# Weight loads of 1, 2 and 1 MB, and the sinks' rows of v from on-chip copies and late loads, in a fused window attention and gated MLP kernel

## The chip, the cores and the metric

The kernel runs on one core of a Trainium2 chip. The metric is device time in microseconds (us) of one execution; lower is better. Times are medians of several executions; the profile comes from one further execution with the hardware profiler on.

## The reference

Attention with a causal window of 128 keys plus 4 "sink" keys at the start of the sequence, over 4 batches, 8 heads, 768 positions and a head size of 64, all float32. Its output, laid out as 3072 tokens by 512, goes through an MLP with a gate.

```python
scores = scale * np.matmul(q, k.transpose(0, 1, 3, 2))
is_sink = pos[None, :] < int(n_sink)
rel = pos[:, None] - pos[None, :]
in_window = (rel >= 0) & (rel < int(window))
scores = np.where(is_sink | in_window, scores, -1000000000.0)
a = np.exp(scores - np.max(scores, axis=-1, keepdims=True))
a = a / (np.sum(a, axis=-1, keepdims=True) + 1e-09)
attn = np.matmul(a, v)
...
x = attn.transpose(0, 2, 1, 3).reshape(B * S, H * D)
h = x @ w_in                       # 3072 x 512 times 512 x 2048
g = h * (1.0 / (1.0 + np.exp(-beta * h)))
out = g @ w_out                    # 2048 x 512
```

## The kernel before, in words

**Units and tiles.** A unit n is one pair of heads over half a sequence (384 queries); there are 32. Four units make a tile of 384 tokens by 512 columns (xT), and there are 8 tiles, two to a batch. For each tile the MLP has 16 blocks of 128 hidden columns. A block is four matmuls (`hidden_matmul`, L814), a tanh on ACT (L822) and a gate on DVE (L835). `project` (L843) then multiplies each block by w_out for three groups of 128 tokens; it can run for two groups at a time.

**A unit's steps.** q and k arrive and are transposed; scores are matmuls (L700, or L727 for later units); the exponential is on ACT (L707, L735), the mask on DVE (L714, L741). In the second half of a sequence the four sink keys lie outside the window for all queries, so there is a separate score matmul against `k_sink` (L670), its exponential `E_sink`, and a matmul with `v_sink` (L759), whose rows 0 to 3 and 32 to 35 hold the first four rows of v for the two heads of the pair. `attend` also multiplies by v (L770), `normalise` makes the reciprocal `rden` (L779) and `o_norm` (L781), and `transpose_out` gives xT.

**Loads.** Each issuing engine has a queue of its own. SP issues q and k of units 0 to 11 as float32 (`load_qk`, L522). ACT issues v of batch 0, first half (L528). GpSimd (POOL) issues all loads that convert float32 to bf16 on the way: w_in in four loads of 1 MB (512 hidden columns each, source rows of 2 KB, L578), w_out in eight of 0.5 MB (L583), the sinks' rows of k (L592) and of v for all batches (two loads of 8 KB, L596), v by half batches (`load_v`, L542), and, from unit 12 on, q, k and v by pair (`land_qk` L552, `land_v` L561). POOL also casts most of the first q, k and v (L621, L532), fills `k_sink` and makes the masks.

**What waits for what around the change.** A load of w_in signals once, at its end; a block that uses any column of it waits for that. `load_qk` for units 4 to 7 waits for the second w_in load. `load_qk` for units 8 to 11 waits for w_out loads (blocks 4, 6, 8 and 10), and `load_v` for batch 1 for other w_out loads. An attention of a second half waits for `v_sink`.

**Order.** The program is written as a list of operations with their reads and writes. A planner (`Prog.order`) works out from given costs (`busy`, `lag`, for a transfer its size over a rate, a `late` offset and a weight for sharing) when each could start, and from that writes one fixed order per engine. Each engine then goes through its order and waits on semaphores; what stands behind a waiting instruction waits too. So a changed cost changes no instruction, but it can change the order. `AGENDA` says at which step (one MLP block is one step) a unit's parts are put on the list, and `products` how many project matmuls a step gets.

Of the kernel before, what the change touches and what calls it, by code (L numbers as in the profile page):

```python
# [9 lines left out]
B, H, S, D = 4, 8, 768, 64  # L10
# [45 lines left out]
AGENDA = {}  # L56
for n in range(4, 8):
    for step, at in (("in", n - 4), ("sink", 16), ("a", 16), ("b", 16), ("av", 17), ("out", 18)):
        AGENDA.setdefault(at if step == "in" else at + 1 * (n - 4), []).append((n, step))
for n in range(8, NU):  # L60
    for at, step in STEPS.items():
        AGENDA.setdefault(FIRST[n] + at, []).append((n, step))
# [294 lines left out]
def bass_streamingllm_window__then__act_swish_beta_kernel(  # L357
# [159 lines left out]
    def load_qk(n, x, after=(), queue="sp"):  # L517
        _, _, half, pb = place(n)
        name = "qk"[x]
        s = rows_of((q, k)[x], n, 1, half, 3)  # L520
        d = stage[name][pb][:, :, 3 * half:3 * half + 3, :].rearrange("p h c d -> p h (c d)")
        op(queue, lambda e: e.dma_start(d, s), w=[(name + "_stage", pb, half)], after=after,  # L522
           dma=f"{name}{pb}_{half}", seq="loads " + queue, **transfer(2 * TT * D * 4, 290 if n not in (1, 2) or x else 170, 520.0))

    def load_v32(x, c):

# [49 lines left out]
    def load_w_in(m, ms, after=()):  # L576
        here = slice(m * 128, (m + ms) * 128)
        op("gp", lambda e: e.dma_start(w_in16[:, :, here], w_in_src[:, :, here]), after=after,  # L578
           w=[("w_in", c, mm) for c in range(4) for mm in range(m, m + ms)],
           dma=f"wi{m}", late=0.0 if m else 800.0, **transfer(DM * ms * 128 * 4, 385, 740.0, 3.0))  # L580

    def load_w_out(m, ms, after=()):
        op("gp", lambda e: e.dma_start(w_out16[:, m:m + ms, :], w_out_src[:, m:m + ms, :]), after=after,  # L583
           w=[("w_out", mm) for mm in range(m, m + ms)],
           dma=f"wo{m}", **transfer(ms * 128 * NOUT * 4, 416, 740.0, 3.0))

    def load_sinks(x, after=()):
        for hh in range(2):
            rows = slice(HEAD1 * hh, HEAD1 * hh + NSINK)
            if x:  # L590
                src = k[:, :, 0:NSINK, :].rearrange("b (g h) s d -> h (b g) s d", h=2)[hh]
                op("gp", lambda e, hh=hh, src=src: e.dma_start(k_rows[:, :, hh, :], src),  # L592
                   w=[("k_rows", hh)], after=after, dma=f"sk{hh}", busy=650.0, lag=300.0, weight=0.4)
            else:
                src = v[:, :, 0:NSINK, :].rearrange("b (g h) s d -> s h (b g) d", h=2)[:, hh]
                op("gp", lambda e, rows=rows, hh=hh, src=src: e.dma_start(v_sink[rows, :, hh, 0:D], src),  # L596
                   w=[("v_sink", hh)], r=["v_sink"], after=after, dma=f"sv{hh}", busy=650.0, lag=400.0, weight=0.4)

    def sink_keys():

# [144 lines left out]
    def attend(n, av_ps=av_ps, name="av"):  # L745
# [9 lines left out]
        with P.together("pe"):  # L755
            for mm in range(3):
                m, at = 3 * half + mm, mm * 2 * D1
                if half == 1:
                    op("pe", lambda e, at=at, mm=mm: e.matmul(  # L759
                        av_ps[:, at:at + 2 * D1], E_sink[z][:, mm * 128:mm * 128 + 128],  # L760
                        v_sink[:, n // 8 * 4 + hp, :, :].rearrange("p h e -> p (h e)"),
                        start=True, stop=False, skip_group_check=True),
                       r=[("E_sink", z), "v_sink", ("v_sink", 0), ("v_sink", 1)], w=[name],
                       **pe(130))
                for hh in range(2):
                    kbs = range(m + 1) if half == 0 else (m - 1, m)
                    for x, kb in enumerate(kbs):
                        col = 128 * where[kb, m]
                        op("pe", lambda e, at=at, hh=hh, kb=kb, col=col, first=(half == 0 and x == 0),
                           last=(x == len(kbs) - 1): e.matmul(  # L770
                            av_ps[:, at + hh * D1:at + hh * D1 + D1], E[z][:, hh, col:col + 128],
                            v_aug[:, pb, hh, kb, 0:D1], start=first, stop=last, skip_group_check=True),
                           r=[("E", z, 0), ("E", z, 1), ("v", pb, kb, hh), ("v_ones", pb)],
                           w=[name], **pe(65))
# [101 lines left out]
    load_w_in(0, 4, [("v", 0, 0, 0)])  # L876
    cast_v(1)
    cast(2)
    load_sinks(1, [("v", 1, 0, 0)])

    select(ident32[:, :], ones32[:, :], [[1, 32]], ALU.is_equal, 0.0, 0, -1, ["ones32"], ["ident32"])
    transpose_first(0)
# [10 lines left out]
    transpose_first(1)  # L893
    first_scores(0)
    cast(3)
    load_w_in(4, 4, [("k16", 0)])
    cast_v(2)
    load_w_in(8, 4, [("v", 2, 0, 0)])
    cast_v(3)
    load_w_in(12, 4, [("v", 3, 0, 0)])  # L900
    for n in range(4):
# [2 lines left out]
        if n < 3:  # L904
            first_scores(n + 1)
        if n == 2:
            for y in range(4, 8):
                for x in range(2):
                    load_qk(y, x, [("w_in", 0, 4)])
            fill("gp", k_sink[:, :, :], 0.0, ["k_sink"], busy=1800.0, after=[("v", 3, 0, 0)])  # L910
            masks([("v", 3, 0, 0)])
            load_sinks(0, [("v", 3, 0, 0)])
            for c in range(3):
                load_v(1, c, [("v", 3, 0, 0)])
            load_w_out(0, 2, [("v", 3, 0, 0)])
# [2 lines left out]
        normalise(n, *bank)  # L918
    for n in range(4):
        transpose_out(n, s_ps[:, n % 2, :], f"s{n % 2}", "dve" if n in (0, 3) else "act")  # L920
    for i in range(2):
        with P.together("pe"):
            for c in range(3):
# [14 lines left out]
    for s in range(-2, S_END + NM):  # L938
# [39 lines left out]
                load_v(2, c, [("w_out", 2 * c + 6)])  # L978
        if s == 23:
            load_v(2, 2)  # L980
        if s in lands:
            for x in range(2):
                land_qk(lands[s], x, [("rden", 0)])
# [57 lines left out]
```

## Time and profile before

| what | value |
|---|---|
| three runs | 229.0 us median, 228.53 to 230.1 |
| the profiled execution's own time | 228.59 us |
| its span, first to last instruction | 226.9 us |
| granted clock of TensorE | 1.0 |
| busy: PE, DVE, ACT, POOL | 220.0, 132.6, 141.3, 125.7 us |
| POOL's waits for a reciprocal before land loads (L552) | 24.0 us, 9 times |
| time to landing, w_in loads: min, median, max | 5.5, 6.8, 9.8 us |
| time to landing, v_sink loads | 7.8 and 7.9 us |
| time to landing, w_out loads: min, median, max | 8.9, 9.6, 11.3 us |

The profile comes from one execution. PE is TensorE's matmul, PEld its weight load, DVE the vector engine, ACT the scalar engine, POOL GpSimd, SP the sync engine; a "q" behind the name means that engine's sequencer, which issues transfers. Times are us from the span's start. A row of the timeline has start, length, engine, source line, operation, tiles as out<-in, the shape and the count; in brackets stands how long the engine was idle before it and what released it. A DMA row on an engine is the issue; the time to landing is counted from that issue to the end of the transfer. A row of stages has its stretch, then busy us and instructions of each engine, the granted clock, the mean share in which the core's 16 DMA engines were busy (over 1 where packets of several queues overlap) and GB/s.

### The profile page before, as it was taken

How to read it: one execution, taken by the hardware profiler on the slowest of the kernel's cores; microseconds unless marked ns; L12 is line 12 of the kernel's file. 1: busy time of each engine (PE TensorE's matmuls, PEld its weight loads, DVE VectorE, ACT ScalarE, POOL GpSimd, SP SyncE). 2: the span in 40 equal slices, each digit the busy share in tenths (PEclk: the TensorE clock that was granted, in tenths of full speed). 3: DMA queues.
4: the chain of work that ended last, by engine and by line, in shares of the span. 5: the costliest groups of instructions: out<-in, count | busy, mean ns of one | idle time of the engine just before them, and what ended most of it. 6: DMA issues, size and time to landing. Idle time of an engine off the chain costs nothing.

```text
span 226.9 us, 4463 instructions
## 1 busy us (share of the span) xinstructions
PE 220.0 (97%) x1761; PEld 122.1 (54%) x1761; DVE 132.6 (58%) x264; ACT 141.3 (62%) x224; POOL 125.7 (55%) x191
## 2 busy tenths in 40 slices
PE   7999989999999999999999999999999999999995
PEld 4665545555555555555555555555555555555454
DVE  5466777488975776566565656555656564443200
ACT  1877796197586877566657766666656755555311
POOL 4689992899994979695939396876300000000000
PEclk9999999999999999999999999999999999999999
DMA  6999999999998999999999999998921012110122
GB/s 172 251 172 179 276 194 205 257 228 139 118 138 124 124 117 151 120 167 144 116 113 135 99 138 147 96 165 119 94 80 53 20 57 64 49 46 0 58 83 92
DMA packets 96901, 28.92 MB, mean 127 GB/s; under 512 B 83424, under 2 KB 93936, under 8 KB 96880
## 3 DMA queue, kind: packets, MB, share of 16 engines
q0 software_dynamic: 59232, 10.92, 65.7%
q1 hardware_dynamic: 34304, 16.79, 34.3%
q10 hardware_dynamic: 3344, 0.93, 1.9%
q8 instruction: 14, 0.23, 0.5%
q14 instruction: 7, 0.06, 0.1%
HBM read 27.34 MB, written 6.29 MB: 148 GB/s over the span
## 4 chain that ended last, share of the span: by engine, by line
PE 73%; DMA 15%; POOL 8%; issue 2%; SPq 1%; ACT 0%; POOLq 0%; ACTq 0%
PE acc L843 32%; PE h_ps L814 29%; DMA k_stage<-in_k_dram 8%; DMA w_out<-in_moe_w_out_dram 4%; PE s_ps L727 4%; PE s_ps L770 4%; POOL qk L621 3%; DMA w_in<-in_moe_w_in_dram 2%; POOL land L552 2%; PE h_ps L843 2%; POOL v_aug L561 1%; PE s_ps L759 1%; PE s_ps L670 1%; SPq L522 1%; POOL v_aug L532 0%
## 5 line engine op out<-in xcount | busy, mean ns | idle before, releaser
L822 ACT ACTIVATE th<-h_ps,beta_half 128x384 f32<-128x384 f32 x120 | 69.4, 581 | 59.7 <-PE h_ps L814 59.1
L843 PE MATMUL acc<-w_out,g 128*128 128x512 bf16 x368 | 99.7, 380 | 0.0
L814 PE MATMUL h_ps<-xT,w_in 128*128 128x384 bf16 x480 | 96.2, 326 | 0.0
L835 DVE SCALAR_TENSOR_TENSOR g<-th,h_ps 128x384 bf16<-128x384 f32 x120 | 65.6, 550 | 44.8 <-ACT th L822 44.0
L814 PEld LDWEIGHTS h_ps<-xT,w_in 128*128 128x128 bf16 x480 | 45.6, 98 | 39.8 <-issue 0.8
L843 PEld LDWEIGHTS acc<-w_out,g 128*128 128x128 bf16 x368 | 32.8, 98 | 28.8 <-issue 3.6
L552 POOL DMA_DIRECT2D land<-in_q_dram x40 | 30.2, 760 | 24.0 <-DVE rden L779 24.0
L552 POOL DMA_DIRECT2D land<-in_k_dram x40 | 30.3, 761 | 0.0
L561 POOL DMA_DIRECT2D v_aug<-in_v_dram x40 | 30.2, 760 | 0.0
L735 ACT ACTIVATE E<-s_ps 128x1536 bf16<-128x1536 f32 x20 | 28.8, 1442 | 0.0
L741 DVE TENSOR_TENSOR E<-E,mask 128x1536 bf16<-128x1536 bf16 x20 | 19.2, 958 | 16.4 <-ACT E L735 16.4
L851 ACT ACTIVATE out_sb<-acc 128x512 f32<-128x512 f32 x23 | 13.7, 596 | 7.6 <-PE acc L843 7.4
L770 PEld LDWEIGHTS s_ps<-v_aug,E 128*128 128x128 bf16 x336 | 15.2, 97 | 3.2 <-issue 1.2
L770 PE MATMUL s_ps<-v_aug,E 128*128 128x65 bf16 x336 | 16.8, 193 | 0.0
L707 ACT ACTIVATE E<-s_ps 128x768 bf16<-128x768 f32 x17 | 13.7, 811 | 4.3 <-PE s_ps L700 4.2
L781 DVE TENSOR_TENSOR o_norm<-s_ps,rden 128x384 bf16<-128x384 f32 x28 | 15.6, 556 | 0.8
L714 DVE TENSOR_TENSOR E<-E,mask 128x768 bf16<-128x768 bf16 x16 | 9.0, 572 | 2.0 <-ACT E L707 1.3
L727 PE MATMUL s_ps<-qkT 64*128 64x256 bf16 (+2 forms) x144 | 10.1, 254 | 0.0
L759 PE MATMUL s_ps<-v_sink,E_sink 128*128 128x130 bf16 x48 | 9.3, 219 | 0.0
L621 POOL CAST qk<-k_stage 128x384 bf16<-128x384 f32 x12 | 6.5, 544 | 4.7 <-DMA k_stage<-in_k_dram 4.4
L673 ACT ACTIVATE E_sink<-s_ps 128x384 bf16<-128x384 f32 x16 | 7.8, 490 | 1.5 <-PE s_ps L670 1.5
L727 PEld LDWEIGHTS s_ps<-qkT 64*128 64x128 bf16 x144 | 4.9, 94 | 7.1 <-issue 5.8
(75 smaller groups left out, 155.2 us busy)
## 6 DMA issues: line engine op xcount, KB each, us to landing
out_dram<-out_sb SPq DMA_DIRECT2D x23, 256.0 KB, 2.7
q_stage<-in_q_dram SPq DMA_DIRECT2D x12, 192.0 KB, 7.4
k_stage<-in_k_dram SPq DMA_DIRECT2D x12, 192.0 KB, 7.9
w_in<-in_moe_w_in_dram POOLq DMA_DIRECT2D x4, 512.0 KB, 6.8
w_out<-in_moe_w_out_dram POOLq DMA_DIRECT2D x8, 256.0 KB, 9.6
land<-in_q_dram POOLq DMA_DIRECT2D x40, 48.0 KB, 3.7
land<-in_k_dram POOLq DMA_DIRECT2D x40, 48.0 KB, 4.0
v_aug<-in_v_dram POOLq DMA_DIRECT2D x40, 48.0 KB, 3.4
```

The lines of the kernel that those rows point to most:

```text
L552: op("gp", lambda e, d=d, s=s: e.dma_start(d, s), w=[("land", pb, half, x, hh)], after=after, dma=f"l{pb}{half}{x}{hh}", **transfer(TT * D ...
L561: op("gp", lambda e, d=d, s=s: e.dma_start(d, s), w=[("v", pb, 3 * half + c, hh) for c in range(3)], after=after, dma=f"lv{pb}{half}{hh}", ...
L707: op("act", lambda e: e.activation(both, src[:, :, 0:TT], AF.Exp, bias=0.0, scale=SCALE), x=list(names), w=[("E", n % NE, c)], **act(768))
L727: op("pe", lambda e, at=at, w=w, kb=kb, qb=qb, nq=nq, hh=hh, rows=rows, bank=bank: e.matmul(s_ps[:, 2 * hh + bank, at:at + w], keys_of(pb, ...
L735: op("act", lambda e: e.activation(E[z][:, :, :], src, AF.Exp, bias=0.0, scale=SCALE), x=list(S_NAMES), w=[("E", z, 0), ("E", z, 1)], **ac ...
L741: op("dve", lambda e: e.tensor_tensor(E[z][:, :, :], E[z][:, :, :], m.unsqueeze(1).to_broadcast([128, 2, 768]), ALU.mult), r=[("E", z, 0), ...
L770: last=(x == len(kbs) - 1): e.matmul(av_ps[:, at + hh * D1:at + hh * D1 + D1], E[z][:, hh, col:col + 128], v_aug[:, pb, hh, kb, 0:D1], sta ...
L781: op("dve", lambda e: e.tensor_tensor(o_norm[o][:, :, :, :].rearrange("p m h d -> p (m h) d"), src[:, :, 0:D], rden[z][:, :].unsqueeze(2). ...
L814: op("pe", lambda e: e.matmul(bank, w_in16[:, c, m * 128:(m + 1) * 128], xT[:, c, T * TT:(T + 1) * TT], start=(c == 0), stop=(c == 3)), r= ...
L822: op("act", lambda e: e.activation(th[i % 3][:, :], bank, AF.Tanh, bias=0.0, scale=beta_half[:, m:m + 1]), x=[name], r=["beta"], w=[("th", ...
L835: op("dve", lambda e: e.scalar_tensor_tensor(g[T % 2][:, m, :], th[i % 3][:, :], 1.0, bank, ALU.add, ALU.mult), r=[("th", i % 3)], x=[name ...
L843: op("pe", lambda e: e.matmul(bank[:, 0:width], g[T % 2][:, m, t * 128:(t + 1) * 128], w_out16[:, m, cols], start=(m == 0), stop=(m == NM ...
```

## The change

The w_in loads become 1, 2 and 1 MB: blocks 0 to 3, blocks 4 to 11 in one load whose source rows are 4 KB, and blocks 12 to 15. The middle load is issued where the second one was. `load_qk` for units 4 to 7 stands later in the program, and still waits for the load that holds block 4, which is now the one of 2 MB. The two loads of the sinks' rows of v for all batches go. For batches 0 and 1, DVE copies the rows from `v_aug`, where v already lies, to `v_sink` (two copies of four partitions by 256 elements for each batch; batch 1 at step 34). For batches 2 and 3, POOL loads them at steps 48 and 80, two small loads each. The sinks' rows of k are loaded as before. Some costs that the planner is given change: the rate of two q loads, the rates of the w_in loads, and the `late` offset of the first.

```diff
--- before.py
+++ after.py
@@ -56,7 +56,7 @@
 AGENDA = {}
 for n in range(4, 8):
     for step, at in (("in", n - 4), ("sink", 16), ("a", 16), ("b", 16), ("av", 17), ("out", 18)):
-        AGENDA.setdefault(at if step == "in" else at + 1 * (n - 4), []).append((n, step))
+        AGENDA.setdefault(at if step == "in" else at + n - 4, []).append((n, step))
 for n in range(8, NU):
     for at, step in STEPS.items():
         AGENDA.setdefault(FIRST[n] + at, []).append((n, step))
@@ -520,7 +520,7 @@
         s = rows_of((q, k)[x], n, 1, half, 3)
         d = stage[name][pb][:, :, 3 * half:3 * half + 3, :].rearrange("p h c d -> p h (c d)")
         op(queue, lambda e: e.dma_start(d, s), w=[(name + "_stage", pb, half)], after=after,
-           dma=f"{name}{pb}_{half}", seq="loads " + queue, **transfer(2 * TT * D * 4, 290 if n not in (1, 2) or x else 170, 520.0))
+           dma=f"{name}{pb}_{half}", seq="loads " + queue, **transfer(2 * TT * D * 4, 290, 520.0))
 
     def load_v32(x, c):
 
@@ -577,24 +577,36 @@
         here = slice(m * 128, (m + ms) * 128)
         op("gp", lambda e: e.dma_start(w_in16[:, :, here], w_in_src[:, :, here]), after=after,
            w=[("w_in", c, mm) for c in range(4) for mm in range(m, m + ms)],
-           dma=f"wi{m}", late=0.0 if m else 800.0, **transfer(DM * ms * 128 * 4, 385, 740.0, 3.0))
+           dma=f"wi{m}", late=0.0 if m else -600.0,
+           **transfer(DM * ms * 128 * 4, 308 if m > 4 else 360, 740.0, 3.0))
 
     def load_w_out(m, ms, after=()):
         op("gp", lambda e: e.dma_start(w_out16[:, m:m + ms, :], w_out_src[:, m:m + ms, :]), after=after,
            w=[("w_out", mm) for mm in range(m, m + ms)],
            dma=f"wo{m}", **transfer(ms * 128 * NOUT * 4, 416, 740.0, 3.0))
 
-    def load_sinks(x, after=()):
+    def load_sink_keys(after=()):
+        for hh in range(2):
+            src = k[:, :, 0:NSINK, :].rearrange("b (g h) s d -> h (b g) s d", h=2)[hh]
+            op("gp", lambda e, hh=hh, src=src: e.dma_start(k_rows[:, :, hh, :], src),
+               w=[("k_rows", hh)], after=after, dma=f"sk{hh}", busy=650.0, lag=300.0, weight=0.4)
+
+    def sink_values(b, eng, after=()):
+
         for hh in range(2):
             rows = slice(HEAD1 * hh, HEAD1 * hh + NSINK)
-            if x:
-                src = k[:, :, 0:NSINK, :].rearrange("b (g h) s d -> h (b g) s d", h=2)[hh]
-                op("gp", lambda e, hh=hh, src=src: e.dma_start(k_rows[:, :, hh, :], src),
-                   w=[("k_rows", hh)], after=after, dma=f"sk{hh}", busy=650.0, lag=300.0, weight=0.4)
-            else:
-                src = v[:, :, 0:NSINK, :].rearrange("b (g h) s d -> s h (b g) d", h=2)[:, hh]
-                op("gp", lambda e, rows=rows, hh=hh, src=src: e.dma_start(v_sink[rows, :, hh, 0:D], src),
-                   w=[("v_sink", hh)], r=["v_sink"], after=after, dma=f"sv{hh}", busy=650.0, lag=400.0, weight=0.4)
+            op(eng, lambda e, rows=rows, hh=hh: e.tensor_copy(
+                v_sink[rows, 4 * b:4 * b + 4, hh, 0:D], v_aug[0:NSINK, :, hh, 0, 0:D]),
+               r=["v_sink", *(("v", z, 0, hh) for z in range(4))], w=[("v_sink", b, hh)],
+               busy=200.0, lag=140.0, after=after)
+
+    def load_sink_values(b):
+        for hh in range(2):
+            rows = slice(HEAD1 * hh, HEAD1 * hh + NSINK)
+            src = v[b, :, 0:NSINK, :].rearrange("(g h) s d -> s h g d", h=2)[:, hh]
+            op("gp", lambda e, rows=rows, hh=hh, src=src: e.dma_start(
+                v_sink[rows, 4 * b:4 * b + 4, hh, 0:D], src),
+               w=[("v_sink", b, hh)], r=["v_sink"], after=[("rden", 0)], dma=f"sv{b}{hh}", busy=650.0, lag=400.0, weight=0.4)
 
     def sink_keys():
 
@@ -760,7 +772,7 @@
                         av_ps[:, at:at + 2 * D1], E_sink[z][:, mm * 128:mm * 128 + 128],
                         v_sink[:, n // 8 * 4 + hp, :, :].rearrange("p h e -> p (h e)"),
                         start=True, stop=False, skip_group_check=True),
-                       r=[("E_sink", z), "v_sink", ("v_sink", 0), ("v_sink", 1)], w=[name],
+                       r=[("E_sink", z), "v_sink", ("v_sink", n // 8, 0), ("v_sink", n // 8, 1)], w=[name],
                        **pe(130))
                 for hh in range(2):
                     kbs = range(m + 1) if half == 0 else (m - 1, m)
@@ -876,7 +888,7 @@
     load_w_in(0, 4, [("v", 0, 0, 0)])
     cast_v(1)
     cast(2)
-    load_sinks(1, [("v", 1, 0, 0)])
+    load_sink_keys([("v", 1, 0, 0)])
 
     select(ident32[:, :], ones32[:, :], [[1, 32]], ALU.is_equal, 0.0, 0, -1, ["ones32"], ["ident32"])
     transpose_first(0)
@@ -893,9 +905,8 @@
     transpose_first(1)
     first_scores(0)
     cast(3)
-    load_w_in(4, 4, [("k16", 0)])
+    load_w_in(4, 8, [("k16", 0)])
     cast_v(2)
-    load_w_in(8, 4, [("v", 2, 0, 0)])
     cast_v(3)
     load_w_in(12, 4, [("v", 3, 0, 0)])
     for n in range(4):
@@ -904,12 +915,9 @@
         if n < 3:
             first_scores(n + 1)
         if n == 2:
-            for y in range(4, 8):
-                for x in range(2):
-                    load_qk(y, x, [("w_in", 0, 4)])
             fill("gp", k_sink[:, :, :], 0.0, ["k_sink"], busy=1800.0, after=[("v", 3, 0, 0)])
             masks([("v", 3, 0, 0)])
-            load_sinks(0, [("v", 3, 0, 0)])
+            sink_values(0, "dve")
             for c in range(3):
                 load_v(1, c, [("v", 3, 0, 0)])
             load_w_out(0, 2, [("v", 3, 0, 0)])
@@ -918,6 +926,9 @@
         normalise(n, *bank)
     for n in range(4):
         transpose_out(n, s_ps[:, n % 2, :], f"s{n % 2}", "dve" if n in (0, 3) else "act")
+    for n in range(4, 8):
+        for x in range(2):
+            load_qk(n, x, [("w_in", 0, 4)])
     for i in range(2):
         with P.together("pe"):
             for c in range(3):
@@ -978,6 +989,10 @@
                 load_v(2, c, [("w_out", 2 * c + 6)])
         if s == 23:
             load_v(2, 2)
+        if s == 34:
+            sink_values(1, "dve", [("rden", 1)])
+        if s in (48, 80):
+            load_sink_values(2 if s == 48 else 3)
         if s in lands:
             for x in range(2):
                 land_qk(lands[s], x, [("rden", 0)])
```

## The prediction

> **What bounds the kernel now.** I read the table by stages first, with its granted clock, then the chain that ended last, then TensorE's and GpSimd's order of time, and last the time to landing of single transfers (a tile's view, narrowed to one issue). Columns of the stages: busy us and instructions of PE, PEld, DVE, ACT, POOL; granted clock; DMA share and GB/s.
>
> ```profile
> 15.00:20.00 5.00, 4.99 (x64) 3.52 (x61) 2.79 (x8) 3.29 (x8) 4.70 (x12) 1.00 1.17 175
> 20.00:25.00 5.00, 5.00 (x32) 2.99 (x32) 4.35 (x9) 4.46 (x9) 5.00 (x11) 1.00 1.17 242
> 25.00:30.00 5.00, 4.59 (x36) 2.42 (x33) 4.05 (x8) 3.51 (x7) 4.88 (x9) 1.00 1.48 245
> 30.00:35.00 5.00, 3.69 (x50) 1.94 (x48) 3.89 (x8) 5.00 (x9) 4.40 (x8) 1.00 1.55 196
> 35.00:40.00 5.00, 5.00 (x62) 2.99 (x58) 3.32 (x8) 2.96 (x5) 0.89 (x1) 1.00 1.24 204
> ```
> The clock is full. TensorE is the bound nearly everywhere after 15 us; the hole that this change can reach is 25 to 35 us, and there the DMA share is 1.48 and 1.55: the DMA engines, not the issuing engines, are full.
>
> ```profile
> 12.45 5.50 DMA w_in<-in_moe_w_in_dram
> 17.96 0.37 SPq L522
> 18.37 7.79 DMA k_stage<-in_k_dram
> ...
> 27.81 9.58 DMA w_out<-in_moe_w_out_dram
> 37.41 0.37 SPq L522
> 37.82 7.45 DMA k_stage<-in_k_dram
> ```
> In the chain the reader is to see that from 12.5 to 45 us transfers alone carry the end: the second weight load lands at 17.95, releases the loads of q and k for units 4 to 7, then w_out (block 4) at 37.39 releases those for units 8 to 11. After 60 us the chain is TensorE and nothing else.
>
> ```profile
> 19.26 1.51 PE L814 MATMUL acc<-xT,w_in 128*128 128x384 bf16 x8
> ...
> 24.51 1.76 PE L814 MATMUL acc<-xT,w_in 128*128 128x384 bf16 x8
> ...
> 34.81 0.34 PE L700 MATMUL h_ps<-qkT 64*128 64x128 bf16 x4 [0.36 <-ACT E L707]
> 35.08 1.04 PE L843 MATMUL acc<-w_out,g 128*128 128x512 bf16 x4
> ```
> Matmuls of L814 start 0.163 us apart, so a block (four) is 0.65. Block 3 starts at 19.26 and block 4, the first that needs the second load, at about 19.9. The second of the two rows from 24.51 on holds block 12's wait for the fourth load (the waits of this window: 0.5 us, once). The first project matmul comes at 35.08.
>
> ```profile
> 12.45 0.76 POOL L578 DMA_DIRECT2D w_in<-in_moe_w_in_dram  x1 [0.30 <-POOL qk L621]
> 14.02 0.74 POOL L578 DMA_DIRECT2D w_in<-in_moe_w_in_dram  x1 [0.30 <-POOL v_aug L532]
> 15.57 0.74 POOL L578 DMA_DIRECT2D w_in<-in_moe_w_in_dram  x1 [0.30 <-POOL v_aug L532]
> 20.92 1.29 POOL L596 DMA_DIRECT2D v_sink<-in_v_dram  x2
> 22.20 2.68 POOL L542 DMA_DIRECT2D v_aug<-in_v_dram  x3
> 24.85 0.74 POOL L583 DMA_DIRECT2D w_out<-in_moe_w_out_dram  x1
> ```
> GpSimd's own queue. Issue plus time to landing gives, in order: w_in 14.4, 17.95, 21.9 and 25.4; v_sink 28.7 and 29.5; v_aug 32.0, 32.8 and 33.6; w_out 34.9, then 36.1 and 37.4. So one stream serves them one behind the other.
>
> **The part before 35 us that is empty.** TensorE's block 15 is through at 28.9 (28.26 plus four times 0.163). From there to 35.08 are 6.2 us, and the starts of the rows in it hold: three sets of six transposes, 0.35 each; six sets of scores, 0.27 each; two sink scores, 0.16 each; one unit's attention, 0.57. That is 3.6 us of work, so 2.6 us are empty for want of w_out, while ACT is busy for 5.00 of 5.00.
>
> **The change, part by part.**
>
> *Second w_in load of 2 MB.* One issue on POOL goes (0.74 and the 0.30 ahead of it: 1.04 us), so everything behind it on POOL moves up by that: the last w_in issue, the fill of k_sink, the masks, v_aug, w_out. None is short of its issue (each lands 8 to 10 us after it), so 0 to the end. What the larger load adds is a wait: blocks 4 to 11 now need all of it. Two loads of 1 MB took from 14.4 to 21.9 (7.5 us); w_out, same rows, lands 0.5 MB of source each 1.28 us, which is 5.1 us for 2 MB. So it lands between 19.6 and 21.9; I take 20.7, about the middle, since no q and k transfers run beside it any more. Block 4 wants it at 19.9: +0.8 us (0 to +2.0) behind which every later block queues. Block 12 loses its wait: −0.5. Block 15 ends 0.3 later, by itself inside the 2.6 empty us, if what follows is not late as well.
>
> The row length is a size for a rule. Spacings of landings are 3.5, 4.0 and 3.5 us per MB although each load takes 5.5 to 9.8 from issue; start-up costs thus lie beside the load in front. The Trainium skill, DMA: Bandwidth & Descriptors, section "Anatomy of one DMA — SWDGE (gpsimd) path", gives about 2.0 us fixed per transfer plus bytes over 436 GB/s. By that, one transfer fewer is 2 us less of stream; by the spacings it is nothing, and I go by the spacings. The result by the rule is the third rival.
>
> *Loads of q and k, units 4 to 7.* They wait for that same load, so SP issues the first at 20.7 and not at 17.96, +2.7. Nothing else waits in SP's queue then (the next is 37.4), so their place in the program is worth 0. They landed first at 25.2 and last at 31.9 (22.52 plus 9.4). The first landing was as late as the fourth w_in load's, 25.4: the engines had been giving themselves to weights. With no q and k beside it that load ends sooner, by about 1 us (four spacings of 3.5 would end at 24.9, at w_out's rate at 22.1). So I take 0 for the landings, ends −0.5 and +2.7 (each time from issue kept as it is).
>
> *v_sink off the queue.* POOL loses 2 issues, 1.29 us: 0, as above. In the stream, the two of 8 KB stand between 25.4 and 29.5, 4.06 us. If that is theirs alone, v_aug and w_out come 4.06 earlier; if the engines were at q and k meanwhile (share 1.48), nothing is won, for those bytes still have to move. Seven of the eight landings of q and k fall in 25.4 to 31.9, so the second is the nearer row: I take 1.0 of the 4.06. First w_out at 33.9, and the project matmuls after it fill what was empty: −1.0 (0 to −2.6, all that is empty). What is late next is w_out's own stream: 1.28 us for two blocks, against four project matmuls of 0.21.
>
> *Two copies of v's rows on DVE for batch 0, two for batch 1.* Nearest row: an xT copy of 384 columns takes 0.35; these have 256, from 4 partitions: 0.25 each. The first two need the last v cast (15.3 now, about 14.2 after), and DVE idles 1.16 us up to 15.24 and 0.51 before 17.52; if they slip behind that, o_norm and so the last xT move by up to 0.5. The other two fall at step 34, where DVE is busy 6.5 of 10 us but TensorE waits for its gate (0.7 us, 3 times in all). Cover gone, 0.5 each; I take +0.2 for both pairs (0 to +1.0).
>
> *Four late DMAs of v_sink rows, steps 48 and 80.* 0.65 each, 1.3 per pair, on POOL, behind a reciprocal that the land loads wait for too. POOL idles 1.3 to 3.8 us there once a unit (24.0 in all, waiting for rden), and land loads come units ahead: 0, or 1.3 late on one unit's loads if that idle is not there.
>
> *The planner's numbers* (rate 290 for q of units 1 and 2, lateness −600, rates 360 and 308) change no instruction, only the order on each engine. Not seen here; bounds ±0.5, one unit's wait like those of 0.5 above; 0 taken.
>
> **Sum.** −1.0 (w_out earlier) +0.3 (block 15 later, taken whole) +0.2 (DVE) = −0.5. The profiled execution took 228.59 (span 226.9 and 1.7 around it), 0.4 under the median 229.0 of the three and at their lower edge: 228.59 − 0.5 = 228.1.
>
> **Rivals.**
>
> *The queue time is really v_sink's.* For: 16 KB can't need 4.06 us of a stream that moves 0.5 MB in 1.28. Against: the share of 1.48. Then w_out starts at about 30.8 and three pairs of blocks, 12 matmuls of 0.21, fill the 2.6 us: 228.59 − 2.6 + 0.3 = 226.3.
>
> *Slower: q and k come late.* Issue moves 2.7 us and landings follow. ACT is full from 29.2 to 36, each unit's cast follows its k within 0.1 us, so there is no slack at the last unit. Work of units 5 to 7 that is now done before 35.08 (two sets of transposes 0.70, four of scores 1.08, a sink score 0.16) then falls behind w_out's arrival: +2.0, with the copies +0.2: 230.8. It decides once k of unit 4 lands after about 27.3 (its cast, transposes and copy take 2 us and block 15 ends at 29.2). For: 2.7 us is more than the 1.1 us that unit 4 has to spare. Against: the first landing has followed the weights, not the issue. The Trainium skill, same page, section "Queues, rings and completion order", has each engine go round its queues by packet, so v_aug, no longer held behind v_sink, would take turns with q and k from the start. By that alone the spacing of q and k landings, 0.95 us, would stretch; in the trace the last three, with v_aug landing beside them, come 0.8 to 1.0 apart, so it does not show.
>
> *Fixed costs are saved.* Stream 2 us shorter: the large load lands at 19.9, block 4 does not wait, block 12's 0.5 goes: 228.59 − 1.0 − 0.5 + 0.2 = 227.3.
>
> **How the numbers follow.** Forecast 0.45, queue time 0.18, late q and k 0.22, fixed costs 0.15. About 1% (2.3 us) is what a measurement can tell from no change. Faster by more than that: the first rival and little else, 0.20. Slower by more: the second rival lies at 1%, so half of it and a little for several ends at once, 0.13. Within: 0.67. The likeliest alone has 227.0 to 229.4; the 8 in 10, reaching to both outer rivals, is 226.0 to 230.9.
>
> **What would show it.** Second w_in landing 6 to 6.5 us after the first and a wait for it at block 4 of 0.5 to 1; no wait at block 12; k of unit 4 landing within 1 us of 26.2; first w_out at 33 to 34.5, first project matmul right behind; the stages 25 to 35 with about 1 us more busy TensorE; stages after 70 us unchanged but for a shift. Wrong if the first project matmul is not earlier, or if TensorE's order before 17 us differs by more than 0.5 us.

## The result, and the profile after

The changed kernel takes 234.26 us (median of six runs, 233.75 to 235.85) against 229.06 for the kernel before (six runs, 227.92 to 230.1): a ratio of 1.0237, with a 95% interval of 1.0205 to 1.0269. It is slower by 5.2 us, outside the range of 226.0 to 230.9. The profiled execution took 233.98 (span 232.2), so the comparison of the two traces has 5.3 us of span to explain. In the experiments below, three of the ten executions of the weights alone (its profiled one among them, 235.3 to 237.5) and one of the eight with the old rate (238.4) lie far above the others of their kernel and are left out of the ratios.

Most lines move by 12: MLP hidden L826, project L855, transposes L646, scores L712, attention L771 and L782, cast L633; the w_out load moves by 1, to L584. The stages of the kernel after, in the same columns:

```profile
15.00:20.00 5.00, 4.99 (x69) 3.31 (x70) 2.50 (x9) 3.44 (x7) 4.73 (x12) 1.00 1.04 178
20.00:25.00 5.00, 5.00 (x32) 2.91 (x31) 3.71 (x7) 4.36 (x8) 5.00 (x9) 1.00 1.28 202
25.00:30.00 5.00, 4.61 (x34) 2.70 (x31) 4.20 (x9) 3.62 (x8) 4.41 (x8) 1.00 1.59 239
30.00:35.00 5.00, 2.58 (x28) 1.39 (x26) 3.25 (x6) 4.29 (x7) 1.11 (x4) 1.00 1.22 229
35.00:40.00 5.00, 3.00 (x27) 1.99 (x29) 1.30 (x4) 2.00 (x4) 3.39 (x6) 0.53 1.24 206
```

From 30 to 40 us TensorE is busy for 5.58 of 10 us, where it was 8.69 before, and from 35 to 40 the granted clock is 0.53. From 15 to 30 us its busy time is as before. All of the loss is there when tile 1 of the MLP begins, at 51.67 and not at 44.51 (7.2 us); 1.9 us of it are made good by the last matmul (229.22 against 223.92). The chain of waits, narrowed to the first 45 us, shows what TensorE stood behind:

```profile
13.26 8.08 DMA w_in<-in_moe_w_in_dram
21.34 0.02 issue
21.35 0.37 SPq L522
...
24.99 11.65 DMA k_stage<-in_k_dram
36.64 0.05 issue
36.70 0.52 POOL qk L633
37.22 0.05 issue
37.26 0.50 PE s_ps L646 x3
...
39.83 1.06 PE acc L855 x2
```

The 2 MB load lands at 21.34, releases SP's loads of q and k, and the last of these (k of unit 7) is issued at 24.99 and lands at 36.64. Then come a cast, the transposes, the scores and the attention ahead of it in TensorE's order, and only then the first project matmul, at 39.83 and not at 35.08. TensorE's own order:

```profile
33.39 0.33 PE L712 MATMUL h_ps<-qkT 64*128 64x128 bf16 x4
35.72 0.48 PE L646 MATMUL s_ps<-ident,qk 128*128 128x128 bf16 x3 [2.01 <-POOL qk L633]
37.26 0.50 PE L646 MATMUL s_ps<-ident,qk 128*128 128x128 bf16 x3 [1.06 <-POOL qk L633]
...
39.83 1.06 PE L855 MATMUL acc<-w_out,g 128*128 128x512 bf16 x2 [0.22 <-issue]
```

The two waits are for the casts of q and k of unit 7. The project matmul has nothing to wait for any more: the first w_out load was issued at 23.27 and landed at 33.9. It stands behind unit 7, and TensorE does not go round it. GpSimd's order shows what was put ahead of the late loads:

```profile
20.64 2.66 POOL L542 DMA_DIRECT2D v_aug<-in_v_dram  x3
23.27 3.54 POOL L584 DMA_DIRECT2D w_out<-in_moe_w_out_dram  x5
26.75 0.57 POOL L633 CAST qk<-q_stage 128x384 bf16<-128x384 f32 x1
...
34.95 0.63 POOL L633 CAST qk<-q_stage 128x384 bf16<-128x384 f32 x1 [2.07 <-DMA q_stage<-in_q_dram]
35.52 0.70 POOL L584 DMA_DIRECT2D w_out<-in_moe_w_out_dram  x1
36.70 0.51 POOL L633 CAST qk<-k_stage 128x384 bf16<-128x384 f32 x1 [0.48 <-DMA k_stage<-in_k_dram]
```

Before, v_aug was issued at 22.20, four microseconds behind the first q (17.96), and w_out, but for its last three loads, one at a time between casts (24.85 to 33.8). Now v_aug goes at 20.64, ahead of the first q (21.35), and five w_out loads follow in one row.

An issue is not yet a first packet. Before, the first q was issued at 17.96 and its first packet moved at 21.60; from 18 to 21 us one queue alone shows packets, that of the weights:

```profile
q0 software_dynamic: 533, 0.53, 112.4%
```

So in packets q and k start only 1.75 us later in the kernel after (23.35 against 21.60), where the issue moved by 3.4. The larger shift is v_aug's: its first packet moves at 23.01, ahead of all of q and k; before, no packet of v_sink or v_aug moved until 25.09.

**How the queues share the DMA engines.** q and k of units 4 to 7 are 8 loads of 256 packets of 768 bytes, on the queue named hardware_dynamic; v_aug (128-byte packets) and the weights (1 KB, 2 KB in the merged load) are on software_dynamic. The transfer view gives packets, MB and share for a stretch. Before, 24 to 25 us, q and k all but alone:

```profile
q1 hardware_dynamic: 413, 0.30, 91.9%
q0 software_dynamic: 36, 0.03, 18.4%
```

After, 31 to 33 us, beside w_out:

```profile
q0 software_dynamic: 282, 0.26, 76.7%
q1 hardware_dynamic: 283, 0.21, 41.5%
```

In one of the experiments (q and k released earlier), 25 to 29 us, beside v_aug:

```profile
q1 hardware_dynamic: 1150, 0.83, 85.0%
q0 software_dynamic: 1150, 0.15, 55.3%
```

Packet for packet: 283 to 282, and 1150 to 1150. q and k move 413 packets per us nearly alone, 288 beside v_aug and 142 beside w_out, whose packets are longer. It is not one to one everywhere: from 24 to 27 us in the kernel after it is 657 of q and k to 1593 of the other queue, 219 per us, which is slower still for q and k; this was not resolved further. So it matters how many of the 2048 are through before the others join. The rule of the Trainium skill, DMA: Bandwidth & Descriptors, section "Queues, rings and completion order", is that each engine goes round its queues by packet. The prediction had set it aside; two of the three stretches beside another queue agree with it, and the third, 657 to 1593, does not.

A share over 1 is no measure of a full rate: before, 24 to 25 us moved 330 GB/s at a share of 1.10, and 28 to 32 us, mostly v_aug, 192 GB/s at 1.88. So the shares of 1.48 and 1.55 from which the prediction called the DMA engines full do not show it by themselves.

### The profile page after: what moved, and what is told of

Read it like the earlier page. It is cut to its first block, busy times and chain, and to the rows that moved or that the text cites. A ratio compares the mean times of both kernels' runs of the same rounds, so it can differ in the third digit from the quotient of the medians.

```text
span 232.2 us, 4436 instructions
## 1 busy us (share of the span) xinstructions
PE 219.8 (95%) x1730; PEld 122.4 (53%) x1757; DVE 133.3 (57%) x268; ACT 141.7 (61%) x224; POOL 127.1 (55%) x192
## 4 chain that ended last, share of the span: by engine, by line
PE 82%; DMA 11%; POOL 2%; issue 1%; SPq 1%; ACTq 1%; ACT 0%; POOLq 0%
PE acc L855 35%; PE h_ps L826 32%; DMA k_stage<-in_k_dram 5%; PE s_ps L782 5%; PE s_ps L739 4%; DMA w_in<-in_moe_w_in_dram 3%; DMA v_stage<-in_v_dram 3%; PE h_ps L855 2%; SPq L522 1%; PE s_ps L712 1%; PE s_ps L771 1%; PE s_ps L682 1%; PE s_ps L646 1%; PE s_ps L810 1%; POOL qk L633 1%
## 5 line engine op out<-in xcount | busy, mean ns | idle before, releaser
L855 PE MATMUL acc<-w_out,g 128*128 128x512 bf16 x341 | 95.4, 382 | 1.5 <-issue 0.5
L826 PE MATMUL h_ps<-xT,w_in 128*128 128x384 bf16 x480 | 96.4, 326 | 0.1
L826 PEld LDWEIGHTS h_ps<-xT,w_in 128*128 128x128 bf16 x480 | 45.5, 98 | 39.4 <-issue 1.0
L855 PEld LDWEIGHTS acc<-w_out,g 128*128 128x128 bf16 x368 | 33.1, 98 | 29.4 <-issue 4.5
L552 POOL DMA_DIRECT2D land<-in_q_dram x40 | 30.6, 767 | 21.9 <-DVE rden L791 21.9
L782 PE MATMUL s_ps<-v_aug,E 128*128 128x65 bf16 x336 | 17.2, 195 | 0.1
L782 PEld LDWEIGHTS s_ps<-v_aug,E 128*128 128x128 bf16 x336 | 15.6, 98 | 3.1 <-issue 1.3
L791 DVE RECIPROCAL rden<-s_ps 128x6 f32<-128x6 f32 x28 | 5.4, 193 | 8.6 <-PE s_ps L782 8.4
L771 PE MATMUL s_ps<-v_sink,E_sink 128*128 128x130 bf16 x48 | 9.6, 223 | 0.0
L633 POOL CAST qk<-k_stage 128x384 bf16<-128x384 f32 x12 | 6.7, 559 | 5.1 <-DMA k_stage<-in_k_dram 5.1
L646 PE MATMUL s_ps<-ident,qk 128*128 128x128 bf16 x48 | 5.0, 230 | 4.6 <-POOL qk L633 4.1
```

The costliest lines, as they stand in the source:

```text
L552: op("gp", lambda e, d=d, s=s: e.dma_start(d, s), w=[("land", pb, half, x, hh)], after=after, dma=f"l{pb}{half}{x}{hh}", **transfer(TT * D ...
L782: last=(x == len(kbs) - 1): e.matmul(av_ps[:, at + hh * D1:at + hh * D1 + D1], E[z][:, hh, col:col + 128], v_aug[:, pb, hh, kb, 0:D1], sta ...
L826: op("pe", lambda e: e.matmul(bank, w_in16[:, c, m * 128:(m + 1) * 128], xT[:, c, T * TT:(T + 1) * TT], start=(c == 0), stop=(c == 3)), r= ...
L855: op("pe", lambda e: e.matmul(bank[:, 0:width], g[T % 2][:, m, t * 128:(t + 1) * 128], w_out16[:, m, cols], start=(m == 0), stop=(m == NM ...
```

## The experiments

**Theories.** *Late q and k:* the release by a load that ends at 21 instead of 18 lets v_aug and w_out be there first; q and k then move at 142 to 288 packets per us, where they had 413, and TensorE waits in order behind unit 7. *The load itself:* one signal for 2 MB holds blocks 4 to 11, and block 15 ends later. *The clock:* the half clock from 35 us on is the loss. *The start:* the planner's new numbers put TensorE's first work in a worse order.

**The parts one by one.** Three runs of the kernel before with one part each. The rate alone:

```diff
-290 if n not in (1, 2) or x else 170, 520.0
+290, 520.0
```

> The kernel before with one planner number of the change alone: the rate of the q loads of units 1 and 2 is 290, not 170. No load and no instruction differs, only the order. Theory A (transfers: q and k of units 4 to 7 land up to 4.8 us late, since they start behind 2 MB of weights and share the DMA engines with v and w_out): this number is worth nothing, 229.1 us. Theory B (order: the planner believes q of unit 1 early, puts unit 1's transposes ahead of unit 0's scores, TensorE waits, its clock falls to 0.80 between 5 and 10 us and the first MLP matmul comes 1.6 us later): 230.7 us, first MLP matmul at about 18.9 instead of 17.3.

Measured: 230.24 against 228.89, ratio 1.0038 (1.0004 to 1.0072). It reorders TensorE's start. Before, from 5.83 us:

```profile
5.83 0.74 PE L450 MATMUL acc<-ones 128*128 128x128 bf16 x5
6.77 0.34 PE L700 MATMUL s_ps<-qkT 64*128 64x384 bf16 x2 [0.21 <-DVE qkT L659]
```

With the rate alone:

```profile
5.83 0.74 PE L450 MATMUL acc<-ones 128*128 128x128 bf16 x5
6.84 0.48 PE L652 MATMUL s_ps<-ident,qk 128*128 128x128 bf16 x3 [0.27 <-DVE qk L621]
7.25 0.50 PE L700 MATMUL s_ps<-qkT 64*128 64x384 bf16 x2
```

Unit 1's transposes stand ahead of unit 0's scores and wait 0.27 us for a cast (in the kernel after the same transposes come at 7.16 and wait 1.03). The MLP begins at 18.24, not at 17.32. By the ratio the rate alone is worth 0.9 us of the 5.2, between the two forecasts. Where these 0.9 us arise is not shown: the profiled execution is the fastest of the ten (227.82), with its last matmul at 223.16, earlier than before.

The weights as 1, 2 and 1 MB, with the later place of the q and k loads, under the old numbers:

```diff
-    load_w_in(4, 4, [("k16", 0)])
+    load_w_in(4, 8, [("k16", 0)])
     cast_v(2)
-    load_w_in(8, 4, [("v", 2, 0, 0)])
...
+    for n in range(4, 8):
+        for x in range(2):
+            load_qk(n, x, [("w_in", 0, 4)])
```

> The kernel before with the weights as 1, 2 and 1 MB and the loads of q and k for units 4 to 7 behind the 2 MB, all planner numbers and the sinks as before. Theory A: k of unit 7 lands 3 us or more after 31.9, TensorE starves between 33 and 38 us: 232 us or more. If only the sinks' part lets w_out run beside q and k, the loads start 2.7 us late but are not slowed further: 230.5 us. Theory B: 229.1 us.

Measured: 228.77 for the seven executions that count (229.44 for all ten), ratio 1.0003 (0.9969 to 1.0037), against theory A's 232 or more. Its profile is of one of the three left out (235.26): v_aug is issued at 21.49, ahead of the first q at 22.57, and k of unit 7 lands at 38.2. So with the weights alone the two issues can cross as well; "no cost" holds for the seven, and what sets the three apart is not shown.

The sinks alone, by DVE copies and late loads:

```diff
-            load_sinks(0, [("v", 3, 0, 0)])
+            sink_values(0, "dve")
...
+        if s == 34:
+            sink_values(1, "dve", [("rden", 1)])
+        if s in (48, 80):
+            load_sink_values(2 if s == 48 else 3)
```

> The kernel before with the sinks' part alone: no early v_sink loads, four copies on DVE, four late small loads; weights, q and k loads and planner numbers as before. My prediction priced this at 0.8 us less: 228.3 us. Theory A in the form that v and w_out, once out from behind v_sink, take engine time from q and k: k of unit 7 lands 1 to 2 us later than 31.9 and the time is 229.5 to 231 us. Theory B: 229.1 us or a little less.

Measured: 229.26, ratio 1.0002 (0.9965 to 1.0039), with the first project matmul where the prediction put it:

```profile
33.99 0.81 PE L854 MATMUL acc<-w_out,g 128*128 128x512 bf16 x3
```

1.1 us earlier than before, and yet no gain: MLP tile 1 begins at 44.98, where it began at 44.51 before.

So by their ratios the parts add up to about 1 us, not to 5.2. The rest of the loss needs more than one of them.

**The parts in pairs.** The kernel after with the old rate (weights and sinks, with the new w_in numbers):

```diff
-290, 520.0
+290 if n not in (1, 2) or x else 170, 520.0
```

> The kernel after with the rate of the q loads of units 1 and 2 back at 170, and nothing else undone. Theory B: the first MLP matmul is back at 17.3 and 1.6 us of the 5.2 come off: 232.6 us; k of unit 7 still lands late. Theory A alone: 234.3 us, since the late loads set the end whatever the start does.

Measured: 230.84, ratio 1.0070 (1.0037 to 1.0102), below both forecasts. The MLP does not go back to 17.3 (it begins at 19.79), so TensorE's start is not what comes back. The planner now issues v_aug at 22.4, behind the first q at 20.7; 1158 packets of q and k are through when v joins, and k of unit 7 lands at 31.7.

The kernel after with four loads of 1 MB again (sinks and new numbers):

```diff
-    load_w_in(4, 8, [("k16", 0)])
+    load_w_in(4, 4, [("k16", 0)])
     cast_v(2)
+    load_w_in(8, 4, [("v", 2, 0, 0)])
```

> The changed kernel with w_in as four loads of 1 MB again (rate 290, the sinks and the place of q and k loads stay). Theory (the release by the 2 MB opens it, v and w_out going ahead of q and k widen it): q and k are issued from about 18, k of unit 7 lands by 33, first project by 36.5, time 229.5 to 230.5. Rival (the planner's numbers and the sinks alone would do, the size of the load does not matter): k of unit 7 still after 35, time over 232.

Measured: 229.56, ratio 1.0041 (1.0009 to 1.0072): as the theory of late q and k had it, and no more than the rate alone. q is issued at 18.5, 1401 packets are through before v joins, k of unit 7 lands at 29.4, and the first project matmul is where it was before:

```profile
35.01 0.81 PE L855 MATMUL acc<-w_out,g 128*128 128x512 bf16 x3
```

The MLP begins at 18.90 here, nearly as late as in the kernel after (18.97), so the late start by itself does not make the loss.

The kernel before with the 1, 2 and 1 MB loads and the rate, v_sink still loaded early:

> The kernel before with the 1, 2 and 1 MB loads, the q and k loads moved behind them, and the rate 290; v_sink is loaded early as before and the w_in numbers are the old ones. Theory: GpSimd still has the two v_sink issues ahead of v_aug and w_out, so q and k keep a lead, k of unit 7 lands between 32 and 35, time 230 to 231.5 where the clock stays up. Rival (the merged load and the order at the start make the loss by themselves, the sinks are innocent): k of unit 7 after 35.5 and 233.5 or more.

Measured: 230.75, ratio 1.0062 (1.0011 to 1.0113), k of unit 7 at 34.7, first project at 37.43, inside the forecast, but not for its reason: q and k keep no lead. v_aug goes only 0.3 us behind the first q and none of their packets is ahead of it, so q and k are slowed here too, but w_out is still issued in part between casts (25.1 to 29.2): about half of the delay, and less than that of the loss.

**The release alone.** The run with four loads, with one token changed: q and k wait for the third load (22.3) and not for the second (18.5). Nothing is merged.

```diff
-            load_qk(n, x, [("w_in", 0, 4)])
+            load_qk(n, x, [("w_in", 0, 8)])
```

> The run with four loads of 1 MB, but q and k of units 4 to 7 are released by the third load (which landed at 21.0 there, as the 2 MB load does at 21.3 in the changed kernel) and not by the second. No load is merged and block 4 waits for nothing new. Theory (the loss is the late release, with v and w_out going ahead): k of unit 7 lands after 35, first project after 38, 233 to 235. Rival (the 2 MB load costs by itself, through block 4's wait and a later end of block 15): k of unit 7 as late or not, time under 231.5.

Measured: 233.64 (median of four), ratio 1.0238 (1.0160 to 1.0316), against 1.0041 with the earlier release. The four executions are far apart: 230.72, 232.96, 234.32 and 235.55, the two lower ones 0.8 and 1.8% above the 228.94 of the kernel before. So the late release costs time with nothing merged, but whether it costs as much as the whole change is not settled. The profiled one is the fastest, and shows less than the expectation said (k of unit 7 at 34.2 and not after 35, first project at 37.43 and not after 38). v_aug is issued at 22.1, ahead of q at 22.3, and 199 packets are through when v joins.

The opposite: the kernel after, merged load and all, with q and k released by the first load:

```diff
-            load_qk(n, x, [("w_in", 0, 4)])
+            load_qk(n, x, [("w_in", 0, 0)])
```

> The kernel after with the loads of q and k of units 4 to 7 released by the first weight load (1 MB) instead of the second (2 MB). Theory A (late start, then sharing): they start at 15.5, share with the weights, all land before 30 us; the 2 MB lands 1 to 2 us later and block 4 waits for it; no clock dip at 35; 230 to 231 us. If the start of these loads has no part in it: 234 us.

Measured: 230.32, ratio 1.0068 (1.0042 to 1.0093). k of unit 7 lands at 30.4, the first project matmul comes at 33.90. In ratios, 1.69 of the 2.37% come back from this alone. The rest is about what the pairs cost. With all the planner's old numbers as well:

> The changed kernel with all of the old planner's numbers and with the q and k loads of units 4 to 7 released by the first w_in load. Theory (with the two openings closed only the late end of block 15 is left): k of unit 7 lands by 31, first project by 34.5, 228.6 to 230. Rival (a residue of 0.7% in the runs with the old rate and with the early release is a cost of its own of the 2 MB load, which keeps block 15 to 30.5 or later): 230.3 to 231.

Measured: 230.11, ratio 1.0053 (1.0020 to 1.0087), between the two forecasts; k of unit 7 at 30.5 and first project at 34.13 as expected. Whether the last half per cent is the merged load's own cost or the order's is not decided by this run. Block 15's last matmul starts at 31.5 here, but also at 29.9 with four loads, 1.2 later than before, so the load is not the only thing that moves it.

**What goes ahead of q and k.** The kernel after with v_aug and w_out held until q of unit 4 has landed:

```diff
-            for c in range(3):
-                load_v(1, c, [("v", 3, 0, 0)])
-            load_w_out(0, 2, [("v", 3, 0, 0)])
...
+    for c in range(3):
+        load_v(1, c, [("q_stage", 0, 1)])
+    load_w_out(0, 2, [("q_stage", 0, 1)])
...
-                load_w_out(m, 2, [("w_in", 0, 0)])
+                load_w_out(m, 2, [("q_stage", 0, 1)])
...
-                load_w_out(m, 2, [("w_in", 0, 8)])
+                load_w_out(m, 2, [("q_stage", 0, 1)])
```

> The kernel after with v of batch 0, second half, and all w_out loads released by the landing of q of unit 4, so that they come behind q and k on the DMA engines; q and k themselves still wait for the 2 MB. Theory A with sharing as the brake: k of unit 7 lands by about 32, no clock dip at 35, 230 to 231 us though w_out lands later. If the wait for the 2 MB is the brake by itself: k of unit 7 still after 34, 233 us or more.

Measured: 231.79, ratio 1.0140 (1.0095 to 1.0184). 1927 of the 2048 packets are through before v joins, and k of unit 7 lands at 29.5, 7.1 us earlier than in the kernel after, although the 2 MB load releases it as there (first q at 20.6). So it is the company, not the release in itself, that makes the loads slow. But only 0.97 of the 2.37% come back: TensorE now waits 1.85 us for a qkT copy on DVE and 0.85 for an exponential, and the first project matmul comes at 36.19. That is a new wait in another place, and the granted clock is at half from 34.15 to 37.56; why those copies are late was not followed further.

The same with w_out alone held back (all its loads), until k of unit 6 has landed:

```diff
-            load_w_out(0, 2, [("v", 3, 0, 0)])
...
+    load_w_out(0, 2, [("k_stage", 2, 1)])
...
```

> The kernel after with the w_out loads alone released by k of unit 6; v of the second half early as in the change. If w_out's 1 KB packets are the brake (they stand beside half of q and k in the trace after): k of unit 7 lands at 32 to 33, 230.5 to 232 us. If v's 128-byte packets are: k of unit 7 still at 35 or later, 233 us or more.

Measured: 232.62, ratio 1.0182 (1.0128 to 1.0235), between the two forecasts. k of unit 7 lands at 33.4, 3.2 of the 7.1 us earlier; but w_out itself is now late (first landing 36.3). Both v_aug and w_out take their part.

**The clock.** The kernel after with 57 extra matmuls on constants in TensorE's order, ahead of the transposes of units 6 and 7, to keep it busy while it waits:

```diff
+            if n in (6, 7):
+                P.pads[P.nodes[-1].id] = {(6, 0): 5, (6, 1): 8, (7, 0): 30, (7, 1): 14}[n, which]
```

> The kernel after with 57 dummy matmuls of 128 columns (0.053 us each) put into TensorE's order where it waits for q and k of units 6 and 7; they write a bank that is free then, and all the rest of the order is as it was. Theory D (clock: the wait between 31 and 37 us makes TensorE's clock fall to 0.5 from 35.3 to 42.1 us, and that costs up to 3.4 us beyond the wait): transfers land as late as before, the clock stays 1.0 after 15 us, 231 to 232 us. Theory A (late transfers are the whole cost and the slow clock only runs beside them): 234 us.

Measured: 234.57, ratio 1.0260 (1.0203 to 1.0316). The stages from 30 us:

```profile
30.00:35.00 5.00, 3.20 (x35) 2.04 (x33) 1.90 (x4) 3.13 (x6) 1.52 (x3) 0.99 1.21 234
35.00:40.00 5.00, 5.00 (x62) 4.39 (x60) 2.67 (x4) 1.51 (x2) 2.70 (x5) 0.67 1.23 211
40.00:45.00 5.00, 4.95 (x63) 2.82 (x61) 2.73 (x7) 3.54 (x6) 1.44 (x2) 1.00 1.18 259
```

The half clock lasts 3.4 us instead of 6.8, and one execution had a mean clock of 1.0; that one still took 233.47. In the profiled one k of unit 7 landed 1.8 us later than in the kernel after, so the times can't be compared as they are. From that landing to tile 1 it takes 13.5 us instead of 15.0, so about 1.5 us may be the clock's, with half of the slow stretch gone. Most of the loss is there without the half clock: the execution at 1.0 was 4.6 us slower than the 228.87 of the kernel before.

**The runs side by side** (profiled executions; packets of q and k moved before v or v_sink joins, counted up to the 51st 128-byte packet; starts of the first project matmul and the last matmul):

| kernel | first q, first v_aug issued | packets ahead | k of unit 7 lands | first project | last matmul | ratio |
|---|---|---|---|---|---|---|
| before | 18.0, 22.2 | 1105 | 31.9 | 35.08 | 223.92 | 1 |
| sinks alone | 18.1, 20.9 | 1164 | 30.7 | 33.99 | 223.57 | 1.0002 |
| rate alone | 17.9, 22.1 | 1200 | 30.8 | 35.16 | 223.16 | 1.0038 |
| four loads | 18.5, 20.7 | 1401 | 29.4 | 35.01 | 223.68 | 1.0041 |
| q, k earlier | 14.4, 19.9 | 778 | 30.4 | 33.90 | 224.95 | 1.0068 |
| early, old numbers | 14.9, 20.3 | 761 | 30.5 | 34.13 | 224.69 | 1.0053 |
| old rate | 20.7, 22.4 | 1158 | 31.7 | 36.34 | 226.08 | 1.0070 |
| weights and rate | 22.2, 22.5 | 0 | 34.7 | 37.43 | 226.68 | 1.0062 |
| four loads, late | 22.3, 22.1 | 199 | 34.2 | 37.43 | 225.94 | 1.0238 |
| after | 21.4, 20.6 | 0 | 36.6 | 39.83 | 229.22 | 1.0237 |

The table has two groups. With a lead of 700 packets or more the loss is 0.7% at most; with less than 200, k of unit 7 lands after 34 and the loss is 0.6 to 2.4%. The row of four loads, late, shows its fastest execution, which is 0.8% above the kernel before and not 2.4%. (The runs that held v_aug or w_out back stand outside, since they delay them by hand, and so does the one with extra matmuls.) The run of weights and rate is the mildest of the second group, and what makes it so beside its spaced w_out loads was not tried.

So the parts work on each other. The merged load takes 3.4 us off the lead of q and k in issues (1.75 in first packets), by their release. Without v_sink and one w_in issue, GpSimd comes to v_aug 1.6 us earlier. The rate changes the planner's order on GpSimd: under the old one v_aug goes at 22.4, with one w_out load issued as early as 15.0; under the new one v_aug goes at 20.6 with five w_out loads behind it. With any two of the three, the end was at most 0.7% late.

## Why the prediction was wrong, step by step

**Second w_in load: right in size.** It landed at 21.34 (taken 20.7, bounds 19.6 and 21.9). Block 4 did not wait for it, because the MLP began 1.65 us later than before (18.97 against 17.32), and block 15 ended 1.4 later, not 0.3. In the run with four loads block 15 is nearly as late (its last matmul starts at 29.94, in the kernel after at 30.16) and the first project matmul comes at 35.01, so this was hidden, as the prediction said of block 15 by itself.

**Loads of q and k: the step that failed.** "I take 0 for the landings", because the first landing "followed the weights, not the issue". The issue moved by 3.4 us (forecast 2.7) and the first k landed only 0.5 later (26.7 against 26.2), so the check that the prediction named was passed. But it took the first landing for all eight: k of unit 7 landed 4.8 later. Forecast 0, bounds −0.5 and +2.7; even the upper bound, the whole shift of the issue, was too small, since it left out that the loads would also move slower. What the runs showed in its place is 4.8 us at the last landing, which TensorE's order hands on to the first project matmul (+4.75, 39.83 against 35.08); with the release by the first load and all else as in the change, that matmul is back at 33.90 and 1.69 of the 2.37% are gone.

**The rival that was right in kind.** "q and k come late" had 0.22 and 230.8. Its mechanism is what happened, but its price was 2.2 us and not 5.2, and its condition (k of unit 4 after about 27.3) was not met, as k of unit 4 came at 26.7: it was unit 7 that mattered. It named the turns by packet and dismissed them because the last three landings, "with v_aug landing beside them, come 0.8 to 1.0 apart". That row could not speak against them: before, q and k were nearly through when v_aug came in force (1940 of 2048 packets by 29 us). What should have been compared is the order of issues. By the prediction's own terms v_aug would move forward by 1.04 and 1.29 us, to about 19.9, and q back to 20.7; the two cross.

**v_sink off the queue: right in its landing, and worth nothing.** The first w_out landed at 33.9, as forecast. In the kernel after the project matmul was not behind it but behind unit 7. In the run with the sinks alone w_out landed at 33.69 and the project matmul began at 33.99 (forecast 33.9), right behind unit 7's attention, and the 1.1 us were gone by tile 1. The forecast of −1.0 to the end was wrong here too. The prediction took 2.6 us between block 15 and the project matmul as empty "for want of w_out". In the trace before, TensorE's matmuls wait 1.2 us in all from 28 to 45 us, and none for w_out (one weight load waits 0.2 us for it):

```profile
PE h_ps L700 <- ACT E L707: 0.6, 2, 0.4
PE s_ps L634 <- ACT qkT L641: 0.4, 1, 0.4
PE s_ps L634 <- DVE qkT L641: 0.2, 1, 0.2
```

So there was little for an earlier w_out to fill. What took the 1.1 us back was not followed.

**DVE copies and late loads of v_sink.** +0.2 and 0, with 1.0002 (0.9965 to 1.0039) for both and the earlier w_out together: no cost is seen. In the kernel after the first two copies took 0.21 and 0.22 us (taken 0.25 each).

**The planner's numbers.** 0, bounds ±0.5. The rate alone costs 0.9 us (0.1 to 1.6); the wait at 7 us is not shown to be the reason. Together with the rest it costs 1.67% (1.0237 against 1.0070), some 3.8 us, since it also decides what GpSimd issues ahead. The text said that TensorE's start could make the forecast wrong; the larger part, by the run with the old rate, was GpSimd's order at 21 to 27 us, which it held to be free of cost ("None is short of its issue ... so 0 to the end").

**Chances.** Slower by over 1% had 0.13. No rival had a half clock, and none had two of the moved issues working on each other.

## What to carry to other kernels

When a load is released later and another is issued earlier, write down both issue times and see whether they cross: here a queue moved 413 packets per us nearly alone and, in two of three stretches beside another, one packet for each of the other's, of 128 bytes or of 1 KB. Ask this of the last transfer of a group, not of the first, and of the engine that consumes them in order. No version here beats the kernel before; the sinks' part alone is level with it.

## What the hardware showed beyond that

TensorE's granted clock went to half in steps of 3.41 us (7.97 to 11.38 after, one step, and 35.28 to 42.10, two; 34.91 to 38.32 with the extra matmuls, one). The Trainium skill, TensorE: Matmul & The Clock Gate, section "Part 1: The HAM clock gate (the "warmup" mystery)", gives a free-running window of 3413 ns, with which the steps agree, and says that an idle window brings the half clock. Here none was wholly idle: the longest wait after 30 us in the kernel after is 2.01 us, and in the run with four loads and the late release the clock went down at 33.52 when the longest wait of the 3.41 us ahead was 1.37; with the weights and the rate it went down at 35.94, and the longest was 0.57.
